# Gated scan and top-1 mixture of experts on one core: the first two pages get their tokens by products with a matrix of ones and zeros, and run on raw fp32 weights

## The chip, the core and the metric

The kernel runs on 1 core of one Trainium2 chip. A core has engines that each run their own list of instructions in order: TensorE (PE, products; its weight loads are PEld), VectorE (DVE), ScalarE (ACT), GpSimd (POOL) and SyncE (SP), which issues most transfers (DMA). The metric is the device time of one execution in microseconds: before the change 928.75 us, the median of 3 runs (927.93 to 928.82).

## The reference

Two stages. The first is a gated linear scan over time, for 4 sequences of 5056 steps and 256 channels; its output is 20224 tokens of 256 numbers. The second sends each token to one of 8 experts.

```python
log_a = c * sig_r * np.log(np.clip(a_base, 1e-06, 1.0 - 1e-06))[None, None, :]
a_t = np.exp(log_a)
norm = np.sqrt(np.maximum(1.0 - a_t * a_t, 1e-06))
x_gated = norm * sig_i * x
for t in range(S):
    h = a_t[:, t] * h + x_gated[:, t]
    y[:, t] = h
...
logits = x @ w_gate + modality_bias[modality_id]
e_idx = np.argmax(logits, axis=1)
...
for e in range(E):
    mask = e_idx == e
    h = np.maximum(x[mask] @ w1[e], 0.0)
    out[mask] = gate_w[mask, None] * (h @ w2[e])
```

An expert is two products, 256 to 1024 and 1024 to 256, with a ReLU between. The bias of the modality decides the expert of nearly every token, so two of the eight experts (the "hot" ones, found on chip from the bias) hold nearly all tokens.

## The kernel before

**Runs.** Time is cut into 23 runs (`RUNS`, called chunks in the code): four of 128 steps, seventeen of 256, and two short ones. A run of 128 steps has 4 x 128 = 512 tokens. For each run: three loads (`load_chunk`: r gate into `a`, i gate into `g`, x into `x`); tanh, exp, square, square root on ACT and the gating on DVE (`scan_chunk`), then the scan itself on DVE (L580); a scale for the run from a sum of squares (`size_chunk`, a small product on PE, L608); a split of the scanned values into a high and a low fp16 half (`split_chunk`, ACT L711 and DVE L714), and the gate logits as products of these halves (PE, L727); the choice of expert and the token's row number (`route_chunk`, DVE, with three small products on PE, L829 to L832: the row number `di` needs how many tokens went to each expert before).

**Rows.** `rows_part` transposes the halves with DMA into a row tile `rt` (SP, L752), one row of 512 fp16 numbers per token with its index and gate value, and POOL scatters these rows to a table `rows` in HBM (L886), 128 tokens a scatter. The table holds each expert's tokens one after the other. A scatter that is recorded after expert products have begun also waits for the PE product recorded last before it (the dependency at the end of `scatter`).

**Pages.** Expert work goes by pages: 256 consecutive rows of one hot expert (later 512, at the end 128). `choose_two` picks one page for each hot expert; `load_rows` reads a page by a transposing DMA (L1206) into `X`, four blocks of 128 x 256 in fp16 (two channel halves, high and low), and the index and gate column into `mt` (L1207). Layer 1 (`first_layer`, L1298) takes, for each block of hidden units, six products of halves (high x high, high x low, low x high, for two channel halves): 48 products of 256 columns a page of 256. ACT and DVE apply the ReLU and split again into `H`; layer 2 (`second_layer`, L1463) is 24 products for each 128 tokens; the result is scaled by the gate and scattered to the output (L1249).

**Weights.** A hot expert's two matrices are loaded in fp32 (`wr`), their scale is worked out (`scale_of`: 16 small products on PE, L339, and one more, L346), and ACT and DVE convert them to a high and a low fp16 half (`convert`, L369 and L375). Pages 0 and 1 (`WHOLE = 2`) are "whole": they keep `H` in fp32 and use the raw fp32 second matrix in layer 2; their first layer uses the fp16 halves.

**What sets the order.** The engines' lists are written by a planner in the program: each piece of work is a generator that asks for an engine for an estimated time, under conditions (`seen`: a mark was reached; `room`: a buffer is free). `run` repeatedly takes the request that can start first, or among near ones that with the best priority (`PRIO`, per run). `PLAN` holds the estimates. `BACKLOG` limits how many tokens the loads run ahead of the pages, `LOOK` and `LOOK_END` how far ahead pages are chosen, `WAIT` when a page is taken up on PE before its data are there, `ROW_STEP` what a later scatter is taken to cost. The planner only sets the order on each engine; on the chip, semaphores set the times.

## Time and profile before

| what | value |
|---|---|
| time, median of 3 runs | 928.75 us |
| the profiled execution's own time | 934.45 us |
| its span | 931.9 us |
| PE busy | 873.1 us, 94% |
| DVE, ACT busy | 662.5 and 662.3 us, 71% each |
| POOL busy | 518.3 us, 56% |
| mean granted clock of PE | 0.991 |

The span is that of the recorded instructions; the execution's time is 2.55 us longer. Busy time says only that an instruction of the engine is under way. The answers of the trace used later are: busy time by stretches, groups of instructions by line (busy us, mean ns of one), the timeline of one engine (start, duration, what), the waits of an engine with what ended them, and the chain of waits that ended last. Where PE's records overlap, the start of one group to the start of the next gives its pace.

### The profile page before, as it was taken

What the parts mean: (1) busy time and instruction counts of PE and PEld (TensorE: products, weight loads), DVE (VectorE), ACT (ScalarE), POOL (GpSimd) and SP (SyncE); (2) the same over time, 40 slices, a digit from 0 to 9 for tenths busy, and PEclk for the clock granted to TensorE, in tenths of its full rate; (3) what the DMA queues carried; (4) which work ended last, traced back from release to release, by engine and by line L of the source; (5) the groups of instructions that cost most, each with busy time, mean ns of one, the idle gap of its engine ahead of it and who ended that gap; (6) DMA issues with size and microseconds to landing.
All of it is one profiled execution on the core that took longest, in us unless ns stands there. A gap on an engine that the chain in (4) does not pass through costs nothing.

```text
span 931.9 us, 22225 instructions
## 1 busy us (share of the span) xinstructions
PE 873.1 (94%) x8453; PEld 775.1 (83%) x8453; DVE 662.5 (71%) x1478; ACT 662.3 (71%) x940; POOL 518.3 (56%) x576
## 2 busy tenths in 40 slices
PE   2399999899799999999999999999999999999996
PEld 2288888798688888888888898888888888888996
DVE  6888687588488778677877887678478667655334
ACT  8977987698688697877888978665376555555343
POOL 5357476578568786776667747755456212221212
PEclk9999999899899999999999999999999999999999
DMA  9999969887776979997798893895473223211230
GB/s 320 235 244 227 234 199 247 216 204 212 212 152 167 284 171 212 219 282 214 199 243 257 193 237 82 182 227 108 104 188 98 63 53 75 52 47 47 58 117 28
DMA packets 223335, 160.96 MB, mean 173 GB/s; under 512 B 197359, under 2 KB 202097, under 8 KB 216690
## 3 DMA queue, kind: packets, MB, share of 16 engines
q1 hardware_dynamic: 206850, 115.20, 53.8%
q0 software_dynamic: 16224, 44.25, 14.6%
q8 instruction: 68, 1.11, 0.5%
q14 instruction: 49, 0.40, 0.1%
q10 hardware_dynamic: 144, 0.00, 0.0%
HBM read 72.96 MB, written 45.01 MB: 127 GB/s over the span
## 4 chain that ended last, share of the span: by engine, by line
PE 84%; issue 5%; DVE 3%; DMA 3%; POOL 2%; ACT 2%; SPq 0%; POOLq 0%; DVEq 0%; ACTq 0%
PE po L1463 42%; PE ph L1298 31%; PE pb L1388 4%; PE pa L1388 3%; PE pc L1388 3%; PE psl L727 2%; DMA wr<-in_moe_w_dram 1%; POOL out_dram L1249 1%; DMA rows<-rt,di 1%; POOL rows L886 0%; DVE x L580 0%; DVE g L554 0%; DMA X<-rows 0%; DVE H L1221 0%; DVE hw L375 0%
## 5 line engine op out<-in xcount | busy, mean ns | idle before, releaser
L1298 PE MATMUL ph<-X,hw 128*128 128x256 f16 (+1 forms) x2880 | 352.4, 273 | 6.2 <-issue 3.8
L1463 PE MATMUL po<-hw,H 128*128 128x256 f16 x2736 | 341.6, 274 | 6.6 <-issue 5.3
L1298 PEld LDWEIGHTS <-hw 128*128 128x128 f16 x2880 | 276.3, 98 | 41.2 <-issue 8.1
L1463 PEld LDWEIGHTS <-H 128*128 128x128 f16 x2784 | 268.7, 98 | 41.1 <-issue 8.2
L886 POOL DMA_INDIRECT rows<-rt,di x158 | 217.2, 1375 | 103.1 <-issue 28.5
L1249 POOL DMA_INDIRECT out_dram<-ot,mt x120 | 146.0, 1217 | 203.2 <-ACT ot L1243 169.9
L1221 DVE SCALAR_TENSOR_TENSOR H<-ph,H 128x512 f16<-128x512 f32 (+1 forms) x240 | 156.4, 667 | 108.0 <-ACT H L1219 82.6
L1219 ACT ACTIVATE H<-ph 128x512 f16<-128x512 f32 (+1 forms) x240 | 137.9, 579 | 117.2 <-PE ph L1298 83.3
L1243 ACT ACTIVATE ot<-po,gt 128x256 f32<-128x256 f32 x160 | 75.1, 472 | 50.8 <-PE po L1463 36.5
L580 DVE TENSOR_TENSOR_SCAN x<-a,x 128x2048 f32<-128x2048 f32 (+2 forms) x23 | 88.1, 3833 | 0.8
L1249 POOL DMA_INDIRECT out_dram<-ot,ids x40 | 49.9, 1248 | 38.3 <-ACT ot L1243 24.6
L1463 PE MATMUL po<-hw,Hx 128*128 128x256 f16 x480 | 68.4, 273 | 0.5 <-ACT Hg L1219 0.5
L566 DVE SCALAR_TENSOR_TENSOR x<-x,g 128x2048 f32<-128x2048 f32 (+2 forms) x23 | 45.9, 1997 | 30.4 <-ACT x L564 22.5
L1463 PE MATMUL po<-hw,Hg 128*128 128x256 f16 x480 | 67.0, 273 | 0.0
L714 DVE SCALAR_TENSOR_TENSOR a<-x,scy,a 128x1024 f16<-128x1024 f32 (+2 forms) x46 | 51.3, 1138 | 2.1 <-ACT a L711 2.1
L1463 PEld LDWEIGHTS <-Hx 128*128 128x128 f16 x480 | 46.8, 98 | 5.9 <-issue 0.6
L1463 PEld LDWEIGHTS <-Hg 128*128 128x128 f16 x480 | 47.0, 98 | 5.4
L1388 PEld LDWEIGHTS <-sw 128*128 128x128 f16 x480 | 47.0, 98 | 5.4
L559 ACT ACTIVATE a<-a,ch 128x1024 f32<-128x1024 f32 (+2 forms) x46 | 50.6, 1119 | 0.1
L711 ACT ACTIVATE a<-x,scy 128x1024 f16<-128x1024 f32 (+2 forms) x46 | 46.1, 1022 | 3.2 <-DVE scy L311 2.0
L554 DVE SCALAR_TENSOR_TENSOR g<-g,x 128x2048 f32<-128x2048 f32 (+2 forms) x23 | 45.8, 1991 | 0.0
L594 ACT ACTIVATE g<-g 128x2048 f32<-128x2048 f32 (+2 forms) x23 | 38.3, 1663 | 4.7 <-DVE x L566 3.4
(226 smaller groups left out, 1110.0 us busy)
## 6 DMA issues: line engine op xcount, KB each, us to landing
a<-in_r_gate_dram SPq DMA_DIRECT2D x17, 1024.0 KB
g<-in_i_gate_dram SPq DMA_DIRECT2D x17, 1024.0 KB
x<-in_x_dram SPq DMA_DIRECT2D x17, 1024.0 KB
wr<-in_moe_w_dram SPq DMA_DIRECT2D x4, 1024.0 KB
cr<-in_moe_w_dram SPq DMA_DIRECT2D x4, 1024.0 KB
a<-in_r_gate_dram SPq DMA_DIRECT2D x5, 512.0 KB
g<-in_i_gate_dram SPq DMA_DIRECT2D x5, 512.0 KB
x<-in_x_dram SPq DMA_DIRECT2D x5, 512.0 KB
```

Of the source, the lines that this page charges most:

```text
L559: nc.scalar.activation(sl, sl, AF.Exp, scale=ch[:, h : h + 1], bias=ch[:, h : h + 1])
L580: nc.vector.tensor_tensor_scan(out=y, data0=a, data1=y, initial=0.0, op0=ALU.mult, op1=ALU.add)
L711: nc.scalar.activation(ys[:, 0, :, u, :], yg[:, :, u, :], AF.Copy, scale=sc)
L714: nc.vector.scalar_tensor_tensor(out=ys[:, 1, :, u, :], in0=yg[:, :, u, :], scalar=sc, in1=ys[:, 0, :, u, :], op0=ALU.mult, op1=ALU.subtract,)
L886: ins = nc.gpsimd.indirect_dma_start(out=rows[:, :], out_offset=bass.IndirectOffsetOnAxis(ap=idx, axis=0), in_=src, in_offset=None, bounds ...
L1219: nc.scalar.activation(hi, src, AF.Relu)
L1221: nc.vector.scalar_tensor_tensor(out=lo, in0=src, scalar=0.0, in1=hi, op0=ALU.max, op1=ALU.subtract)
L1243: nc.scalar.activation(ot, po, AF.Copy, scale=t.gt[:, a : a + 1])
L1249: ins = nc.gpsimd.indirect_dma_start(out=out[:, :], out_offset=bass.IndirectOffsetOnAxis(ap=t.mt[:, a, 0:1] if t.ids is None else t.ids[:, ...
L1298: ins = nc.tensor.matmul(ph[:, v, 0:st], lhsT, rhs, start=(m == 0 and v == 0), stop=(m == len(mm) - 1), skip_group_check=True,)
L1388: ins = nc.tensor.matmul(to[:, v, :], lhsT[s], rhs[x], start=(i in (1, 7) and v == 0 and m == 0), stop=(m == 2), skip_group_check=True,)
L1463: ins = nc.tensor.matmul(prev.po, prev.h(hx, f, rs_), wv[:, wx, f], start=(prev.count == 1), stop=(prev.count == products))
```

## The change

The first run's tokens reach pages 0 and 1 without the table in HBM.

- `choose_pages` now begins with a `choose_two` for run 0 alone, as soon as its tokens have row numbers; before, the first pages were chosen once the scatter of run 0's rows was planned to be done.
- `gather` builds `X` of these pages on chip. For each of the run's 4 columns of 128 tokens, DVE compares the token's place in the page with the numbers 0 to 255 (`place`, a new constant), which gives a 128 x 256 fp16 matrix `to` of ones and zeros. PE multiplies the row tile `rt` with it: 4 products a column (two halves, two channel blocks), 16 a page, summed in one bank, so that high and low are added up. ACT copies the bank to `X`, now 2 blocks in fp32.
- `load_places` still reads index and gate (`mt`) from the table, once run 0's rows are there. The transposing loads `X0` and `X1` fall away.
- Layer 1 of pages 0 and 1 uses the raw fp32 matrix `wr0` or `wr2`: 16 fp32 products a page for 48 fp16 ones. The raw matrix is kept until then, and the gate column is only copied, not scaled.
- `convert` of the four hot matrices stays, for the later pages. The row tile of run 0 is kept until the gathers are done.
- The planner's numbers are others: those below, most of `PRIO` and of `PLAN`. A temporary tile `tie` moves to another pool.

All other pages do the same work; the number of pages and their sizes are as before. Two plain products of 512 columns come in where a bank is first written near the end (`pb`, L1388 before).

The order moves as follows. On DVE, behind the routing of run 0 (`dt0`, `di0`: its row numbers; `x1`: run 1's gating and scan; `hw0_1`: conversion of a second matrix). Before:

```order
L840 TENSOR_TENSOR dt0_479<-psl0_343,be_186 128x32
L845 TENSOR_TENSOR dt0_479<-dt0_479,oh0_457 128x32
L849 TENSOR_REDUCE di0_482<-dt0_479 128x4
L853 TENSOR_TENSOR be_186<-be_186,psl0_343 128x8
L566 SCALAR_TENSOR_TENSOR x1_306<-x1_306,g1_298 128x1024
L375 SCALAR_TENSOR_TENSOR hw0_1_218<-wr1_308,sc1_381,hw0_1_218 128x1024
L574 TENSOR_TENSOR fed1_508<-a1_287,last0_357 128x8
L428 TENSOR_TENSOR hiv0_221<-iv0_320,iv1_382 128x1
L576 TENSOR_TENSOR x1_306<-x1_306,fed1_508 128x8
L578 MEMSET a1_287 128x8
L580 SCALAR_TENSOR_TENSOR x1_306<-a1_287,x1_306 128x1024
```

In the change:

```order
L586 SCALAR_TENSOR_TENSOR x1_310<-a1_291,x1_310 128x1024
L380 SCALAR_TENSOR_TENSOR hw0_1_223<-wr1_337,sc1_403,hw0_1_223 128x1024
L589 COPY last1_518<-x1_310 128x8
L434 TENSOR_TENSOR hiv0_226<-iv0_314,iv1_404 128x1
L312 TENSOR_SCALAR scy1_516<-psl1_513 128x1
L316 TENSOR_SCALAR scy1_516<-scy1_516 128x1
L318 TENSOR_SCALAR ivy1_517<-scy1_516 128x1
L621 TENSOR_TENSOR ivl1_524<-ivy1_517,ivg_233 128x1
L849 TENSOR_TENSOR dt0_527<-psl0_348,be_186 128x32
L854 TENSOR_TENSOR dt0_527<-dt0_527,oh0_442 128x32
L858 TENSOR_REDUCE di0_530<-dt0_527 128x4
L862 TENSOR_TENSOR be_186<-be_186,psl0_348 128x8
```

The row numbers of run 0 stood ahead of run 1's gating and scan; they now stand behind the scan and behind the second half of a conversion. The selection and the eight compares `to` follow them.

On PE, at the first page (`pt3`: scale of the fourth matrix; `psl1`: routing of run 1; `ph0_*`: page 0's layer 1). Before:

```order
L829 MATMUL psl1_525<-oh1_651,um1_163 128x32
L830 LDWEIGHTS ones_161
L830 MATMUL psl1_525<-cu1_653,ones_161 128x32
L832 LDWEIGHTS ones_161
L832 MATMUL psl1_525<-cu1_653,ones_161 128x8
L346 MATMUL pt3_629<-ss3_628,onesf_153 128x1
L608 LDWEIGHTS onesb_157
L608 MATMUL psl2_712<-ssy2_662,onesb_157 128x1
L608 LDWEIGHTS onesb_157
L608 MATMUL psl2_712<-ssy2_662,onesb_157 128x1
L1298 LDWEIGHTS hw0_0_217
L1298 MATMUL ph0_0_747<-X0_0_682,hw0_0_217 128x256
```

In the change:

```order
L838 LDWEIGHTS um1_163
L838 MATMUL psl1_513<-oh1_722,um1_163 128x32
L839 LDWEIGHTS ones_161
L839 MATMUL psl1_513<-cu1_724,ones_161 128x32
L841 LDWEIGHTS ones_161
L841 MATMUL psl1_513<-cu1_724,ones_161 128x8
L1370 MATMUL ph0_1_759<-X0_0_563,wr0_269 128x256 x4
L351 MATMUL pt3_729<-ss3_707,onesf_153 128x1
L1370 MATMUL ph0_2_783<-X0_0_563,wr0_269 128x256 x4
L1370 MATMUL ph0_3_796<-X0_0_563,wr0_269 128x256 x4
L1370 MATMUL ph1_0_814<-X1_0_579,wr2_473 128x256 x4
L1542 MATMUL po0_0_835<-wr1_337,H0_677 128x256 x4
```

Page 0's first layer began behind the routing of run 1; it now begins ahead of it (`ph0_0` stands 20 products ahead of `ph0_1`, of which 17 are for the scales), and the rest of it comes behind the three routing products. Layer 2 of page 0 (`po0_0`) begins, as before, after the first group of page 1.

On SP, before, the part with page 0's load (`rt1`: transposes of run 1; `X0`, `mt0`: page 0's tokens and places):

```order
L752 DMA_TRANSPOSE rt1_0_599<-a1_287 128x4x128 x4
L1201 TENSOR_LOAD sel1_579
L1201 ISA x2
L1206 ISA
L1206 DMA_TRANSPOSE X0_0_682<-rows_78 128x4x256
L1207 ISA
L1207 DMA mt0_681<-rows_78 128x2x2
L522 DMA x3_708<-in_x_dram 128x1024
```

In the change, the part with page 2's load:

```order
L1240 DMA mt1_720<-rows_78 128x2x2
L758 DMA_TRANSPOSE rt1_0_616<-a1_291 128x4x128
L528 DMA g3_747<-in_i_gate_dram 128x1024
L528 DMA x3_774<-in_x_dram 128x1024
L528 DMA a4_830<-in_r_gate_dram 128x2048
L1265 TENSOR_LOAD sel2_841
L1265 ISA x2
L1270 ISA
L1270 DMA_TRANSPOSE X2_0_866<-rows_78 128x4x256
L1271 ISA
L1271 DMA mt2_865<-rows_78 128x2x2
L528 DMA g4_878<-in_i_gate_dram 128x2048
```

Ahead of the last transpose of run 1 there are now the two reads of places, `mt0` and `mt1`, which need run 0's rows in the table; behind it stand three loads and then page 2's tokens, `X2`.

```diff
-WAIT = 2.0
+WAIT = 6.0
...
-BACKLOG = 9000
-LOOK = 256
-LOOK_END = 2944
+BACKLOG = 10500
+LOOK = 384
+LOOK_END = 2432
...
-W_AT = [5, 2, 4, 2]
+W_AT = [10, 3, 6, 2]
...
-ROW_STEP = 2.4
+ROW_STEP = 1.6
...
@@ -209,6 +209,11 @@
     islot = const.tile([P, 2], I32, name="islot")
     nc.gpsimd.iota(islot, pattern=[[P, 2]], base=0, channel_multiplier=1)
     nc.gpsimd.tensor_copy(slot, islot)
+    iplace = sm.tile([P, P], I32, name="iplace", tag="jk", bufs=1)
+    nc.gpsimd.iota(iplace, pattern=[[1, P]], base=0, channel_multiplier=0)
+    place = const.tile([P, 256], F16, name="place")
+    nc.gpsimd.tensor_copy(place[:, 0:P], iplace)
+    nc.gpsimd.tensor_scalar(out=place[:, P:256], in0=place[:, 0:P], scalar1=float(P), scalar2=None, op0=ALU.add)
     pidx = const.tile([P, 1], I32, name="pidx")
     nc.gpsimd.iota(pidx, pattern=[[0, 1]], base=0, channel_multiplier=1)
     quarter = const.tile([P, 1], F32, name="quarter")
...
+            yield "SP", 0.0, seen(("raw1", e)), 0.0
...
-                    rh = rt.bitcast(F16)
+                    rh = tiles["rh", c] = rt.bitcast(F16)
...
             scatter(f"rows{c}", rt[:, u, 0:ROW], di[:, PART * j + u : PART * j + u + 1])
+        end = plan["end"]
+        mark["put", c, j] = end + (PLAN["put"] if c < PLAN["exact"] else 3.0)
+        if c == 0:
+            yield "SP", 0.0, seen(*[("placed", e) for e in range(HOT)]), 0.0
         give("rt", tr)
...
-    def choose_two(size, full, last=False):
+    def choose_two(size, full, last=False, c=None):
 
 
         sel, ticket = new_sel()
-        b2 = tiles["b2", routed(plan["end"]) - 1]
+        b2 = tiles["b2", routed(plan["end"]) - 1 if c is None else c]
...
     def choose_pages():
         other, at = None, FAR
         summed = lambda: max(mark.get(("sw", e), FAR) for e in range(HOT))
+        yield "DVE", 0.16, allof(seen(("route", 0)), room("sel")), 0.0
+        yield from choose_two(256, True, True, 0)
         look = lambda: drained(count["chosen"] - (LOOK if summed() >= FAR else LOOK_END))()
         while True:
...
@@ -1182,6 +1195,51 @@
         yield "POOL", 0.2, None, 0.0
         nc.gpsimd.tensor_tensor(out=t.ids, in0=m, in1=t.mt[:, :, 0], op=ALU.add)
 
+    def gather(t):
+
+        C, r = columns(0), t.pg.e
+        yield "DVE", 0.16, room("X"), 0.0
+        at = sm.tile([P, C], F32, name=f"at{t.n}", tag="at")
+        nc.vector.scalar_tensor_tensor(
+            out=at, in0=t.pg.d[:, r : r + 1].broadcast_to([P, C]), scalar=-256.0, in1=tiles["di", 0], op0=ALU.mult, op1=ALU.add
+        )
+        t.tx.append(take("X"))
+        t.X.append(pm.tile([P, 2, 256], F32, name=f"X{t.n}_0", tag="X", bufs=BUFS["X"]))
+        oh = []
+        for c in range(C):
+            yield "DVE", 0.17, None, 0.0
+            oh.append(sm.tile([P, 256], F16, name=f"to{t.n}_{c}", tag="to", bufs=4))
+            nc.vector.tensor_scalar(out=oh[-1], in0=place, scalar1=at[:, c : c + 1], scalar2=None, op0=ALU.is_equal)
+        for c in range(C):
+            yield "PE", 0.45, allof(room("ph"), seen(("tr", 0, 0))) if c == 0 else None, 0.2 if c == C - 1 else 0.0
+            if c == 0:
+                tp, bank = take_bank(f"pg{t.n}", True)
+            for x in range(2):
+                for k in range(2):
+                    nc.tensor.matmul(
+                        bank[:, k, :], tiles["rh", 0][:, c, x * D + k * P : x * D + (k + 1) * P], oh[c],
+                        start=(c == 0 and x == 0 and k == 0), stop=(c == C - 1 and x == 1), skip_group_check=True,
+                    )
+        mark["placed", r] = plan["end"]
+        if free["ACT"] <= free["DVE"]:
+            yield "ACT", 0.59, None
+            nc.scalar.activation(t.X[0], bank, AF.Copy)
+        else:
+            yield "DVE", 0.68, None
+            nc.vector.tensor_copy(t.X[0], bank)
+        give("ph", tp)
+        t.ready = plan["end"]
+
+    def load_places(t):
+
+        pg, na = t.pg, t.pg.st // P
+        yield "DMA", 0.3, seen(*[("put", 0, j) for j in range(parts(0))]), 0.2
+        src = nc.sync.value_load(pg.sel[0:1, pg.col : pg.col + 1], min_val=0, max_val=NULLS + WIDE - pg.size)
+        sel_read(pg)
+        t.mt = pm.tile([P, na, 2], I32, name=f"mt{t.n}", tag="mt", bufs=10)
+        read_rows(pg, nc.sync.dma_start(t.mt, rows[ds(src, pg.st), D:].rearrange("(a p) m -> p a m", p=P)))
+        mark["places", t.n] = plan["end"]
+
     def load_rows(n=0):
         while True:
             while n >= len(pages):
@@ -1189,7 +1247,13 @@
                     return
                 yield "SP", 0.0, lambda: 0.0 if len(pages) > n or count["ended"] else FAR, 0.0
             pg = pages[n]
-            if True:
+            if n < HOT:
+                t = Tile()
+                t.pg, t.n, t.X, t.tx, t.ready, t.ids = pg, f"{pg.n}", [], [], FAR, None
+                queue.append(t)
+                add(gather(t), (0, 3), plan["end"], urgent=True)
+                add(load_places(t), (0, 2), plan["end"])
+            else:
                 st, na = pg.st, pg.st // P
                 t = Tile()
                 t.pg, t.n, t.X, t.tx = pg, f"{pg.n}", [], []
...
         if t.pg.e is None:
             return max(t.ready, mark.get(("cw", t.pg.c), FAR))
+        if t.pg.n < HOT:
+            return max(t.ready, mark.get(("got", 2 * t.pg.e), FAR))
...
             tp, ph = take_bank(f"ph{cur.n}_{g}", st == 256)
-            w1v = (pg.w if pg.e is None else hw[pg.e])[0].rearrange("p (s k f) -> p s k f", s=2, k=2)
+            if pg.n < HOT:
+                wf = raw2[pg.e, 0][0].rearrange("p (k f) -> p k f", k=2)
+            else:
+                w1v = (pg.w if pg.e is None else hw[pg.e])[0].rearrange("p (s k f) -> p s k f", s=2, k=2)
             for v in range(2):
                 f = 2 * g + v
                 fs = slice(f * P, (f + 1) * P)
-                mm = [
-                    (w1v[:, s, k, fs], cur.X[0][:, 2 * x + k, :])
-                    for k in range(2) for s, x in ((0, 0), (0, 1), (1, 0))
-                ]
+                if pg.n < HOT:
+                    mm = [(wf[:, k, fs], cur.X[0][:, k, :]) for k in range(2)]
+                else:
+                    mm = [
+                        (w1v[:, s, k, fs], cur.X[0][:, 2 * x + k, :])
+                        for k in range(2) for s, x in ((0, 0), (0, 1), (1, 0))
+                    ]
                 for m, (lhsT, rhs) in enumerate(mm):
...
             for g in range(4):
-                yield 1.312 * st / 256, [room("ph")] + ([ready, room("H")] if g == 0 else []), lambda g=g: plain(g), 0.25
+                yield 1.75 if pg.n < HOT else 1.312 * st / 256, [room("ph")] + ([ready, room("H")] if g == 0 else []), lambda g=g: plain(g), 0.25
...
             if begins:
                 conds.append(room("po"))
+                if prev.pg.n < HOT:
+                    conds.append(seen(("places", prev.n)))
                 if a // 2 not in prev.to:
                     conds.append(room("ot"))
                 if pg.e is not None and not prev.to:
-                    conds.append(seen(("got", 2 * pg.e + 1), ("w", 2 * pg.e)) if prev.whole else seen(("hot", pg.e)))
+                    conds.append(seen(("got", 2 * pg.e + 1), *([] if pg.n < HOT else [("w", 2 * pg.e)])) if prev.whole else seen(("hot", pg.e)))
             yield "PE", (0.45 if prev.whole else 0.328) * len(run_), allof(*conds), 0.0
             if not prev.to:
                 gates = prev.mt[:, :, 1].bitcast(F32)
                 prev.gt = sm.tile([P, st // P], F32, name=f"gt{prev.n}", tag="gt", bufs=3)
-                nc.vector.tensor_scalar(out=prev.gt, in0=gates, scalar1=pg.inv if pg.e is None else tiles["wiv", 2 * pg.e] if prev.whole else hiv[pg.e], scalar2=None, op0=ALU.mult)
+                if pg.n < HOT:
+                    nc.vector.tensor_copy(prev.gt, gates)
+                else:
+                    nc.vector.tensor_scalar(out=prev.gt, in0=gates, scalar1=pg.inv if pg.e is None else tiles["wiv", 2 * pg.e] if prev.whole else hiv[pg.e], scalar2=None, op0=ALU.mult)
             if begins:
                 if a // 2 not in prev.to:
                     prev.to[a // 2] = take("ot")
```

More of the change, by code (lines that the diff above doesn't have):

```diff
@@ L54 @@
 EARLY = 7
-ROW_STEP = 2.4
+ROW_STEP = 1.6
 LAG = 2.5
-PLAN = dict(dma=3.6, b0=0, b1=16, b2=0, b3=24, put=1.5, hold=1, cold=20, ls=4.4, lr=0.14, ll=0.16, lc=0.36, dma0=0.5, l1=12, l4=24, exact=9, w0=6, w1=4, w2=4, w3=6, land=2, xland=3, row=1.55, beside=9, op=0.13, gprio=0, oh=0.1, lag=1.5, latefrom=8, h=(0, 0), o=(0, 4))
+PLAN = dict(dma=3.6, b0=5.6, b1=20, b2=8.4, b3=20, put=1.5, hold=1, cold=5, ls=4.4, lr=0.09, ll=0.16, lc=0.42, dma0=1.0, l1=12, l2=20, l3=34, l4=28, exact=5, w0=6, w1=3, w2=6, w3=6, land=2, xland=3, row=1.3, beside=9, op=0.13, gprio=0, oh=0.1, lag=2, latefrom=8, h=(0, 0), o=(0, 4), convkey='route', convhold=(1, 0, -1, -1), sumhold=(0, 1, -1, 1))
 def lag_of(c):
@@ L147 @@
     cmp = const.tile([1, E, E], F32, name="cmp")
-    tie = const.tile([1, E, E], F32, name="tie")
+    tie = sm.tile([1, E, E], F32, name="tie", tag="ex")
     nc.vector.tensor_tensor(out=tie, in0=keyt.broadcast_to(one8), in1=key.broadcast_to(one8), op=ALU.is_equal)
@@ L774, in rows_part @@
             scatter(f"rows{c}", rt[:, u, 0:ROW], di[:, PART * j + u : PART * j + u + 1])
+        end = plan["end"]
+        mark["put", c, j] = end + (PLAN["put"] if c < PLAN["exact"] else 3.0)
+        if c == 0:
+            yield "SP", 0.0, seen(*[("placed", e) for e in range(HOT)]), 0.0
         give("rt", tr)
-        mark["put", c, j] = plan["end"] + (PLAN["put"] if c < PLAN["exact"] else 3.0)
     def route_chunk(c):
@@ L1031, in choose_two @@
             pg = new_page(size, e, sel, e, not full)
+            if c is not None:
+                pg.routed, pg.d = c + 1, d
             pg.ticket = ticket, left
@@ L1304, in plain @@
             if g == 3:
+                if pg.n < HOT:
+                    mark["raw1", pg.e] = plan["end"]
                 for tx in cur.tx:
@@ L1444, in second_layer @@
                 prev.gt = sm.tile([P, st // P], F32, name=f"gt{prev.n}", tag="gt", bufs=3)
-                nc.vector.tensor_scalar(out=prev.gt, in0=gates, scalar1=pg.inv if pg.e is None else tiles["wiv", 2 * pg.e] if prev.whole else hiv[pg.e], scalar2=None, op0=ALU.mult)
+                if pg.n < HOT:
+                    nc.vector.tensor_copy(prev.gt, gates)
+                else:
+                    nc.vector.tensor_scalar(out=prev.gt, in0=gates, scalar1=pg.inv if pg.e is None else tiles["wiv", 2 * pg.e] if prev.whole else hiv[pg.e], scalar2=None, op0=ALU.mult)
             if begins:
```

2 lines of the change are left out of this document (1 added, 1 removed).

## The prediction

> **What bounds the kernel now.** I read the busy times first, then the same by stretches, then TensorE's waits, then the chain of waits.
>
> ```profile
> PE 873.1 (94%) x8453; PEld 775.1 (83%) x8453; DVE 662.5 (71%) x1478; ACT 662.3 (71%) x940; POOL 518.3 (56%) x576
> ```
>
> TensorE (PE) is busy for 94% of the span. By stretches (us; busy time of PE, PEld, DVE, ACT, POOL; then granted clock, DMA share, GB/s):
>
> ```profile
> 0.00:48.00 48.00, 13.09 (x119) 10.92 (x120) 35.85 (x123) 42.86 (x53) 23.27 (x100) 1.00 0.94 273
> 48.00:81.00 33.00, 33.00 (x255) 28.17 (x255) 27.88 (x72) 27.14 (x36) 19.57 (x25) 1.00 0.93 239
> 162.00:176.00 14.00, 10.71 (x94) 8.02 (x93) 6.49 (x17) 6.90 (x9) 7.75 (x13) 0.76 0.90 227
> 249.00:924.00 675.00, 667.95 (x6559) 597.79 (x6558) 478.43 (x1036) 460.70 (x690) 362.51 (x329) 1.00 0.62 154
> 924.00:932.00 8.00, 0.33 (x4) 0.05 (x1) 0.00 (x0) 0.47 (x1) 0.98 (x1) 0.79 0.06 17
> ```
>
> PE idles for 35 us before 48, then hardly at all until 924. Its waits say the same (line, what ended the wait: us, times, longest):
>
> ```profile
> PE psl L727 <- issue: 5.2, 9, 1.2
> PE ph L1298 <- DMA X<-rows: 2.2, 1, 2.2
> PE po L1463 <- DVE H L1221: 1.1, 2, 0.6
> ```
>
> Once, at page 0, it waits for tokens. So a change of the start is worth what it moves PE's unbroken stretch, less the PE work it puts into that stretch. The chain of waits into page 0 (start, us, what):
>
> ```profile
> 35.85 1.97 POOL rows L886
> 38.13 6.39 DMA rows<-rt,di
> 44.53 3.40 DMA X<-rows
> 47.97 8.36 PE ph L1298 x60
> ```
>
> The last scatter of run 0, its 6.39 us to land and the 3.40 us load are what the change takes out.
>
> **The change, part by part.** *PE's prices.* PE's timeline:
>
> ```profile
> 39.26 1.87 PE L339 MATMUL pt<-wr 128*128 128x128 bf16 x16
> 56.16 1.89 PE L1463 MATMUL po<-wr,H 128*128 128x256 f32 x8
> 57.89 1.47 PE L1298 MATMUL ph<-X,hw 128*128 128x256 f16 x12
> 59.20 1.89 PE L1463 MATMUL po<-wr,H 128*128 128x256 f32 x8
> 75.01 0.55 PE L727 MATMUL psl<-wg,a 128*128 128x16 f16 x16
> 80.34 1.47 PE L1298 MATMUL ph<-X,hw 128*128 128x256 f16 x12
> ```
>
> Start to start, four fp32 products (eight records) take 57.89 - 56.16 = 1.73 us, 0.433 each; twelve fp16 ones 59.20 - 57.89 = 1.31, 0.109 each. Layer 1 of the two pages: 96 x 0.109 = 10.5 us go, 32 x 0.433 = 13.9 come. The gathers add 32 x 0.109 = 3.5, the two plain products of 512 columns near the end 4 x 0.109 = 0.4.
>
> *A cold PE.* Groups of page 0's products in 49 to 50 and in 52.6 to 53.4 us (busy, mean ns):
>
> ```profile
> L1298 PE MATMUL ph<-X,hw 128*128 128x256 f16 x6 | 1.5, 421 | 0.0
> L1298 PE MATMUL ph<-X,hw 128*128 128x256 f16 x10 | 1.3, 272 | 0.0
> ```
>
> The first products go at half pace: 60 took 8.36 us instead of 6.5. I take the same 1.8 us for the gathers, which come first in the change; the 32 column-sum products behind them then cost half of row 39.26's pace, 1.75 us together. The Trainium skill (TensorE: Matmul & The Clock Gate, section "What's actually happening") says that the array's clock is halved after an idle window and released after about 3.4 us of sustained work, a time and not a number of products. That speaks against the change, which puts more products into the cold time; by it the gathers lose about 1.7 us, and without it the start would come out that much better. The trace agrees: half pace from 47.97 to about 51.4.
>
> *When the gathers begin.* The DVE's and ACT's rows:
>
> ```profile
> 25.99 1.13 ACT L369 ACTIVATE hw<-wr,sc 128x1024 f16<-128x1024 f32 x1
> 28.44 1.15 ACT L564 ACTIVATE x<-x,quarter 128x1024 f32<-128x1024 f32 x1
> 29.14 0.21 DVE L849 TENSOR_REDUCE di<-dt 128x4 int32<-128x32 f32 x1
> 29.62 1.23 DVE L566 SCALAR_TENSOR_TENSOR x<-x,g 128x1024 f32<-128x1024 f32 x1 [0.20 <-ACT x L564]
> 30.76 1.28 DVE L375 SCALAR_TENSOR_TENSOR hw<-wr,sc,hw 128x1024 f16<-128x1024 f32 x1
> 32.38 2.44 DVE L580 TENSOR_TENSOR_SCAN x<-a,x 128x1024 f32<-128x1024 f32 x1
> ```
>
> Run 0's row numbers are ready at 29.4 before; the change puts them behind run 1's scan and a conversion. On ACT the root of run 1 now stands ahead of the conversion of row 25.99, so the gating of row 29.62 comes about 1.5 us earlier, at 28.1. From there: gating 1.15, conversion 1.2, small steps 0.4, scan 2.3, conversion 1.2, six scale steps 0.7, row numbers and totals 1.0, selection 0.6, place 0.15: 36.8. A compare of 128 x 256 is not in the trace; below it lies a compare-sized step of 128 x 16 elements, above it half of one of 128 x 512:
>
> ```profile
> 10.29 0.23 DVE L661 TENSOR_SCALAR wg<-wg,scg 128x16 f16<-128x16 f32 x1
> 59.40 0.69 DVE L1232 TENSOR_SCALAR H<-ph 128x512 f32<-128x512 f32 x1 [1.52 <-PE ph L1298]
> ```
>
> So 0.1 (a small step's start-to-start share) to 0.35 us each; I take 0.2, nearer the small one, since the operands are fp16 in SBUF. The first gather begins at **37.0**; with no gain on ACT and slow compares at 39, with quick small steps at 36. The eight compares (1.6 us) hide behind the gathers (5.3 us), or at 0.35 nearly so.
>
> *From there to the end of page 2's layer 1* PE has: gathers 3.5 + 1.8; column sums 1.75 and two closing products 0.4; logits of runs 1 and 2 0.8; small products 0.2; fp32 layers 1 and 2 of both pages 13.9 + 13.9; page 2's layer 1 48 x 0.109 = 5.2. Sum 41.4, so 78.4. The routing of run 1 that now stands inside page 0 needs DVE until about 45.5, and PE reaches it at 46.4, so it costs only its products. ACT's copy of a bank (0.6) hides behind the column sums. Before, that point is 80.34, less 0.45 for run 3's logits and routing, which the change has later: 79.9. **The start gains 1.5 us; less 0.4 for the two products, 1.1.** With the bounds of the gathers' begin: -0.9 to +2.1. Dropping two of 82 page loads and the two adds on POOL frees nothing that PE waited for; the longer lives of `wr0`, `wr2` and `rt0` delay no load that is not already issued.
>
> *What is late next.* Page 2's tokens. Their scatters each wait for the product recorded before them, the last one for the end of page 1's first group, in the list above four fp32 groups after the routing; POOL's and SP's rows of run 1 before:
>
> ```profile
> POOL rows L886 <- PE ph L1298: 25.5, 26, 2.1
> 52.49 1.84 POOL L886 DMA_INDIRECT rows<-rt,di  x1 [0.30 <-issue]
> 59.57 1.25 SPq L1206 DMA_TRANSPOSE X<-rows  x1
> ```
>
> Last scatter to page load 7.1 us, plus 3.4 to land: 10.5. PE has seven fp32 groups, 12.1 us, between the same two points, a margin of 1.6. But SP's list also holds the last transpose of run 1 behind `mt0`, which needs run 0's rows: scatters from 36.3 to about 41.8, landing 6.4, two reads 0.9, the transpose about 3.4 give 52.5 for run 1's first scatter, against 48.1 by the products; then page 2 is 1.8 late. I take the middle, 0, as both orders of events are possible.
>
> The planner's other numbers move runs and loads by a few groups in the middle, where PE waits for no run; I take 0. The profiled execution (934.45) lies 5.7 above the median, so its stalls are not all in the timed runs: I set the sum on the median, 928.75 - 1.1 = **927.6**.
>
> **The rivals.**
>
> *A. A stall of the middle goes.* SP's list before run 6:
>
> ```profile
> 151.74 0.35 SPq L522 DMA_DIRECT2D a<-in_r_gate_dram  x1
> 152.19 0.38 SPq L522 DMA_DIRECT2D g<-in_i_gate_dram  x1
> 158.87 7.95 SPq L752 DMA_TRANSPOSE rt<-a  x4
> ```
>
> In 162 to 176 (row above) PE did about 6.1 us of work in 13.1: waits that nothing in the profile ends, then half clock; DVE and ACT stand at half too. SP had just issued two loads of 1024 KB ahead of run 6's transposes; the change moves one behind them. For it: the place; against: other such stretches lie where nothing moves. If the half clock alone goes (24 products at twice 0.109: 2.6), 925.0; if all 6.9 goes, 920.7. I say 923.5.
>
> *B. The row numbers come sooner.* If DVE reaches them at 34 instead of 36 (each of some fifteen small steps 0.1 us quicker than I count) and PE's routing of run 1 is no later, another 1.5 us: 926.1.
>
> *C. Page 2's or page 4's tokens are late.* Page 4 before:
>
> ```profile
> 85.44 1.25 SPq L1206 DMA_TRANSPOSE X<-rows  x1
> 96.26 4.09 PE L1298 MATMUL ph<-X,hw 128*128 128x256 f16 x36
> ```
>
> Run 2's last scatter now stands behind page 2's second layer; by the same count page 4 is left with 10.6 us of PE work for 10.5 of transfers. With 2 us more for a landing at both places PE waits 1.8 + 2 at the first and 2 at the second: 5.8 - 1.1, **933.4**. It decides from 3 us of waits on. Against it: before, page 4's load was issued 10.8 us ahead of its use, so it was ready some 7 us early. That the early pages bring nothing at all, as `X` is early but page 2 takes all of it back, is the forecast's upper end, 928.8.
>
> **How the numbers follow.** Forecast 0.38, A 0.25, B 0.17, C 0.20. What this kernel's measurement tells from no change is 0.2%, 1.9 us. Forecast (its own range 926.6 to 929.6) is "same" up to its ends; A and B are faster, C slower. So faster 0.42, same 0.37, slower 0.21. The predicted time is the forecast's, 927.6. The range takes in B, A's middle and its far end nearly, and C's first place alone (928.75 - 1.1 + 3.8 = 931.5): 921.0 to 931.5.
>
> **What would show it.** First gather at 36 to 39 and the end of page 2's layer 1 near 78.4; gathers at 421 ns, then 272; no PE wait on `X<-rows` over 1 us. For A, no clock below 0.9 near 162 to 176. For B, the first gather before 36. For C, PE waiting for `X<-rows` at pages 2 or 4. The forecast is wrong if PE is not unbroken from the gathers on, or if the time moves while the end of page 2's layer 1 does not.

## The result, and the profile after

The changed kernel takes **940.77 us** (median of 4 runs, 938.09 to 942.59) against 928.79 for the kernel before (4 runs, 927.93 to 929.92): ratio 1.0139, 95% interval 1.0095 to 1.0183. It is 12 us slower. The forecast was 927.6, and its range ended at 931.5. Below, an execution that lay far above the others of its kernel is left out of median and ratio.

TensorE's busy time and records in the page after:

```profile
PE 880.9 (94%) x8455; PEld 779.1 (83%) x8455; DVE 664.4 (71%) x1488; ACT 662.8 (71%) x942; POOL 519.5 (55%) x575
```

TensorE by three stretches that are the same in both (us; busy time and records, granted clock, DMA share, GB/s), first before, then after:

```profile
48.00:81.00 33.00, 33.00 (x255) 1.00 0.93 239
81.00:120.00 39.00, 38.03 (x373) 1.00 1.02 252
120.00:705.00 585.00, 569.79 (x5613) 0.99 0.81 198
```

```profile
48.00:81.00 33.00, 33.00 (x210) 1.00 0.86 226
81.00:120.00 39.00, 34.78 (x342) 0.96 0.87 209
120.00:705.00 585.00, 567.35 (x5576) 0.99 0.81 203
```

Up to 81 us TensorE is unbroken, as forecast. Then come two places that the forecast left at nothing: 4.2 us of idle time between 81 and 120 (before: 1.0), and 17.7 between 120 and 705 (before: 15.2, in an execution that lay 5.7 us above the median). TensorE's waits after the start (what ended them; us, times, longest) say what kind they are:

```profile
PE po L1542 <- issue: 7.0, 16, 1.0
PE ph L1370 <- issue: 4.5, 8, 1.3
PE po L1542 <- DVE H L1285: 3.4, 2, 2.0
PE psl L838 <- DVE oh L827: 1.0, 1, 1.0
```

The `issue` rows are stalls that no wait explains. The other two are true waits; but for 1.3 us behind 400 us they lie in the first stretch. The timeline of TensorE, ACT and DVE there (start, duration, what; in brackets the idle time ahead of it and what ended it):

```profile
36.71 5.38 PE L1219 MATMUL pg<-to,rt 128*128 128x256 f16 x32 [5.64 <-DVE to L1212]
78.48 1.47 PE L1370 MATMUL ph<-X,hw 128*128 128x256 f16 x12
92.49 0.39 PE L1542 MATMUL po<-hw,H 128*128 128x256 f16 x2 [0.93 <-ACT x L570]
94.94 4.86 PE L1542 MATMUL po<-hw,H 128*128 128x256 f16 x28 [2.05 <-DVE H L1285]
```

```profile
89.95 2.00 ACT L570 ACTIVATE x<-x,quarter 128x2048 f32<-128x2048 f32 x1
91.86 0.58 ACT L1283 ACTIVATE H<-ph 128x512 f16<-128x512 f32 x1
```

```profile
91.99 2.29 DVE L572 SCALAR_TENSOR_TENSOR x<-x,g 128x2048 f32<-128x2048 f32 x1 [1.33 <-ACT x L570]
94.19 0.68 DVE L1285 SCALAR_TENSOR_TENSOR H<-ph,H 128x512 f16<-128x512 f32 x1
```

The start went as worked out: the first gather at 36.71, and the last group that the sum counts ends where the next begins, at 78.48 (forecast 78.4). At 92 us TensorE wants the last quarter of page 3's hidden layer. Its rectifier stands behind run 4's square root in ACT's list and its second half behind run 4's gating in DVE's, so TensorE gets it at 94.9. Behind the two waits the 28 products take 4.7 us, start to start, in place of 3.1. The Trainium skill (TensorE: Matmul & The Clock Gate, section "What's actually happening") says that an idle window halves the array's clock until it has been busy again for about 3.4 us; the granted clock of 0.96 over this stretch agrees.

### The profile page after: what moved, and what is told of

Same layout as the page of the kernel before. It is cut to its first block, busy times and chain, and to the rows that moved or that the text cites. A ratio compares the mean times of both kernels' runs of the same rounds, so it can differ in the third digit from the quotient of the medians.

```text
span 940.0 us, 22221 instructions
## 1 busy us (share of the span) xinstructions
PE 880.9 (94%) x8455; PEld 779.1 (83%) x8455; DVE 664.4 (71%) x1488; ACT 662.8 (71%) x942; POOL 519.5 (55%) x575
## 5 line engine op out<-in xcount | busy, mean ns | idle before, releaser
L1542 PE MATMUL po<-hw,H 128*128 128x256 f16 x2736 | 345.3, 275 | 11.9 <-issue 7.0
L1370 PE MATMUL ph<-X,hw 128*128 128x256 f16 (+1 forms) x2784 | 339.4, 272 | 4.8 <-issue 4.5
L1370 PEld LDWEIGHTS <-hw 128*128 128x128 f16 x2784 | 265.8, 98 | 38.7 <-issue 7.8
L895 POOL DMA_INDIRECT rows<-rt,di x158 | 220.2, 1394 | 104.7 <-issue 36.2
```

The source lines that it names most:

```text
L895: ins = nc.gpsimd.indirect_dma_start(out=rows[:, :], out_offset=bass.IndirectOffsetOnAxis(ap=idx, axis=0), in_=src, in_offset=None, bounds ...
L1370: ins = nc.tensor.matmul(ph[:, v, 0:st], lhsT, rhs, start=(m == 0 and v == 0), stop=(m == len(mm) - 1), skip_group_check=True,)
L1542: ins = nc.tensor.matmul(prev.po, prev.h(hx, f, rs_), wv[:, wx, f], start=(prev.count == 1), stop=(prev.count == products))
```

## The experiments

Up to four kernels at a time ran on one chip, with the kernel before on the same chip. A single edit is shown against the changed kernel unless it says otherwise.

**The same two kernels on other chips.** e5 is the kernel before, e6 and e12 are the changed kernel, none of them edited.

> The kernel before once more, unchanged, for a trace from the chip on which these runs are made: the comparison of traces so far is between two profiled executions of another chip, and there the one of before lay 5.7 us over its own median, with two stalls of 7 and 8.5 us at 162 and 232 us that no wait explains. If those stalls belong to that chip or that execution, this trace has none and PE's waits add to less than 5 us after the start; if they belong to the kernel, they stand at the same places.

> The changed kernel once more, unchanged, beside the kernel before on this chip. Ratio 1.010 to 1.018 if the loss is the kernel's own. If the loss of the first comparison came from stalls without a wait (13.6 us of PE's idle time in its trace), which the other chip hardly shows, the ratio is 1.000 to 1.008.

> The changed kernel once more beside the kernel before, for the chip on which the next two are made. If the loss of the first comparison (12 us) belongs to that chip, the ratio is 1.002 to 1.004 again; if it depends on the hour or on chance, it can be anywhere from 1.002 to 1.018, and then this trace has stalls of TensorE that no wait explains.

| chip | kernel before, us | changed kernel, us | ratio, 95% interval |
|---|---|---|---|
| of the first comparison | 928.79 | 940.77 | 1.0139 (1.0095 to 1.0183) |
| of e5 to e7 (e15, e16 later: 909.32 before) | 909.25 | 911.45 | 1.0028 (1.0018 to 1.0037) |
| of e12 to e14 | 925.98 | 937.39 | 1.0132 (1.0109 to 1.0155) |
| of e1 to e4 / e8 to e11 / e17, e18 | 909.01 / 909.57 / 909.46 | not run | |

Chips differ: on a quicker one (909 us) the loss is 2.2 us, on a slower one (926 to 929) 11 to 12. The first comparison does not name its chip, so it may be that of e12 to e14. The trace on the quicker chip separates the two causes, since it has no stall without a wait. TensorE by stretches, e5 and then e6:

```profile
81.00:120.00 39.00, 39.00 (x387) 1.00 0.99 264
120.00:705.00 585.00, 584.53 (x5836) 1.00 0.84 201
```

```profile
81.00:120.00 39.00, 35.55 (x364) 1.00 0.83 205
120.00:705.00 585.00, 584.56 (x5836) 1.00 0.83 206
```

Nothing is lost behind 120 us, in either kernel. The 3.45 us between 81 and 120 are the changed kernel's own. Of these the start gives back about 1. The waits of e6 that make them up:

```profile
93.30 3.23 PE L1542 MATMUL po<-hw,H 128*128 128x256 f16 x28 [1.29 <-DVE H L1285]
104.74 0.51 PE L733 MATMUL psl<-wg,a 128*128 128x16 f16 x14 [1.01 <-DVE a L720]
111.52 0.19 PE L838 MATMUL psl<-oh,um 128*128 128x64 f16 x1 [1.01 <-DVE oh L827]
```

All three wait on run 4: for the group held up behind its gating, for its scaled values (its logits), for its choice of expert. In the trace after, the first of them is 2.98 us in two parts, with half clock behind it: there ACT stands 1.50 us for a product of TensorE ahead of run 4's root, which e6 does not show.

**Numbers or structure.** e1 is the changed code with all of the planner's numbers as before, e2 the code before with all of the new numbers, e3 and e4 take back one table each.

```diff
e1  WAIT, BACKLOG, LOOK, LOOK_END, W_AT, PRIO, ROW_STEP, PLAN: as before
e2  (kernel before) the same eight: as in the change
e3  PRIO: as before
e4  PLAN: as before
```

> The changed kernel with all of the planner's numbers (WAIT, BACKLOG, LOOK, LOOK_END, W_AT, PRIO, ROW_STEP, PLAN) as they were before; the gathers, the raw fp32 layers and the early routing of run 0 stay. Theory N (the numbers cost the time: the order that they give ACT, DVE and SP after the start makes PE wait, first for the last group of page 3's first layer): the loss is gone, 926 to 930. Theory S (the new work itself costs it: gathers, fp32 layers, the rows of run 0 held on chip): still 938 to 942. Under a mixture, where the numbers fit the new start and the old ones do not, it is slower than 930 for a reason of its own, and PE's waits show at another place.

> The kernel before with all of the changed planner's numbers and nothing else of the change. Theory N: most of the 12 us comes with the numbers, 937 to 943. Theory S: 927 to 931, as the kernel before.

> The changed kernel with the table PRIO alone as before. Theory N, with the table as the main number, since it sets which run's steps stand ahead of a page's first layer on DVE and ACT: 927 to 933. If the numbers of PLAN carry it, or theory S: 937 to 943. The static order still has run 4's gating ahead of the last group of page 3 on DVE, so a wait of PE for H of about 5 us near 90 us can stay.

> The changed kernel with the dictionary PLAN alone as before (the planner's costs and due times of loads). Theory N with PLAN as the main number: 927 to 933. If PRIO carries it, or theory S: 937 to 943. Here DVE has run 4's gating ahead of the last but one group of page 3.

| kernel | time, us | ratio, 95% interval |
|---|---|---|
| e1, new code, old numbers | 943.55 | 1.0375 (1.0361 to 1.0389) |
| e2, old code, new numbers | 931.26 | 1.0249 (1.0235 to 1.0263) |
| e3, old PRIO | 924.00 | 1.0170 (1.0151 to 1.0189) |
| e4, old PLAN | 918.35 | 1.0096 (1.0081 to 1.0112) |

Neither theory N nor S, but the third case of e1's expectation: every mixture is slower than the changed kernel's 1.0028 on such a chip. The numbers and the code fit each other, and a misfit costs more than the change does. In e1 the next page's tokens are late, by rival C's mechanism: TensorE stands for them for 15 us.

```profile
125.51 4.85 PE L1370 MATMUL ph<-X,hw 128*128 128x256 f16 x22 [15.34 <-DMA X<-rows]
```

The mixtures also show what each part does to run 4. Its gating on DVE, in e5 (old code, old numbers), e1 (code alone), e2 (numbers alone) and e6 (both):

```profile
83.83 2.29 DVE L566 SCALAR_TENSOR_TENSOR x<-x,g 128x2048 f32<-128x2048 f32 x1 [0.97 <-ACT x L564]
```

```profile
86.55 2.29 DVE L572 SCALAR_TENSOR_TENSOR x<-x,g 128x2048 f32<-128x2048 f32 x1 [2.62 <-ACT x L570]
```

```profile
92.26 2.29 DVE L566 SCALAR_TENSOR_TENSOR x<-x,g 128x2048 f32<-128x2048 f32 x1 [2.99 <-ACT x L564]
```

```profile
90.35 2.29 DVE L572 SCALAR_TENSOR_TENSOR x<-x,g 128x2048 f32<-128x2048 f32 x1 [1.82 <-ACT x L570]
```

The code alone makes it 2.7 us later, the numbers alone 8.4, both 6.5. So each part makes it later, but they do not add up, and the share of each in the change stays open. What the code adds can be read from e6 at the start. ACT's and DVE's rows:

```profile
40.31 0.60 ACT L1226 ACTIVATE X<-pg 128x512 f32<-128x512 f32 x1 [4.91 <-PE pg L1219]
40.81 0.81 ACT L565 ACTIVATE a<-a,ch 128x512 f32<-128x512 f32 x1
46.33 1.15 ACT L570 ACTIVATE x<-x,quarter 128x1024 f32<-128x1024 f32 x1
```

```profile
37.75 0.29 DVE L1212 TENSOR_SCALAR to<-place,at 128x256 f16<-128x256 f16 x1 [0.58 <-PE pg L1219]
40.52 1.41 DVE L720 SCALAR_TENSOR_TENSOR a<-x,scy,a 128x512 f16<-128x512 f32 x2
```

ACT stands 4.9 us for the first page's bank, with run 2's exponentials queued behind it; run 2's root comes at 46.3, where e5 has it at 40.4:

```profile
40.42 1.15 ACT L564 ACTIVATE x<-x,quarter 128x1024 f32<-128x1024 f32 x1
```

DVE stands four times for 0.53 to 0.58 us, because the second page's compares wait for the four buffers of the first, with run 1's scaling behind them. No run takes away ACT's wait, so that it is what makes run 4 later is argued and not shown.

**Run 4.** e7 and e8 exchange two pairs of neighbours, so that page 3's group goes ahead of run 4; all other rows stay. In e7 run 4's squares of g also overtook the gating, which then worked on squared values; e8 keeps the computation.

```diff
 ACT
+H3<-ph3_3
 x4<-x4,quarter      (root)
-H3<-ph3_3
 DVE
+H3<-ph3_3,H3
 x4<-x4,g4           (gating)
-H3<-ph3_3,H3
```

> The changed kernel with two pairs of neighbours exchanged and every other row of every engine's list as it was: on ACT the rectifier of page 3's last group goes ahead of run 4's square root, on DVE the same group's rest goes ahead of run 4's gating. Theory Q (PE stands at 92 us because this group waits in ACT's and DVE's lists behind run 4): the waits of 0.9 and 2.05 us and the half clock behind them go, 3 to 5 us less than the changed kernel beside it, and PE's progress at 100 us is as at 80 us. Theory R (the time comes back at the next late step, since run 4's scan is no earlier): 0 to 2 us less, and the wait for the routing of run 4 near 113 us grows from 1.0 us to 3 to 5 us.

> The exchange of the run before this one with the computation kept: on ACT the rectifier of page 3's last group goes ahead of run 4's root, on DVE the same group's rest ahead of run 4's gating, and run 4's squares stay behind the gating, which they had lost; all other rows of all lists stand as in the changed kernel. On a chip like the last the changed kernel lies 2.2 us over the one before (0.28%). Theory Q (page 3's group is held up by its place in the lists): PE's wait of 1.3 us at 93 us goes and with it 1.3 to 2 us of the time. Theory R (run 4 itself is late: its root, gating, scan and scaling end when they end, and PE stands for its logits and its routing next): the wait at 93 goes, those at 104 and 111 us (1.0 each) grow by as much, and the time is the changed kernel's within 0.5 us.

e7: 916.01 us, ratio 1.0076 (1.0063 to 1.0089), not a clean measure. e8: 913.81 us, 1.0048 (1.0035 to 1.0061). Theory Q falls: the wait for the group went, and others came, for run 4 again:

```profile
97.62 0.16 PE L619 MATMUL psl<-ssy,onesb 128*128 128x1 bf16 x1 [1.22 <-ACT g L605]
107.12 0.51 PE L738 MATMUL psl<-wg,a 128*128 128x16 f16 x14 [1.18 <-DVE a L725]
```

In e8 ACT stands 1.59 us for page 3's products ahead of run 4's root, and run 4's gating begins at 93.24 where e6 has it at 90.35; 0.7 us of this stands ahead of it already. So this exchange only hands the delay on to run 4. It is even 0.2% slower than the changed kernel, where theory R expected the same time.

e9 shortens run 4's chain, e10 lengthens it, e14 lengthens it in the kernel before.

```diff
e9, run 4 only
-sqrt(x4); x4 = max(x4, ..) * g4
+sqrt(x4[first half]); sqrt(x4[second half])
+x4[first half] = max(..) * g4; x4[second half] = max(..) * g4
e10, e14, run 4 only
+nc.scalar.activation(y, a, AF.Square)
 nc.scalar.activation(y, a, AF.Square)
```

> The changed kernel with run 4's root and gating each issued as two halves, so that DVE gates the first half while ACT takes the root of the second: run 4's scan starts about 1.0 us sooner at 0.1 to 0.2 us more work on each engine; nothing else moves. Theory R (run 4's chain sets PE between 88 and 112 us): 0.7 to 1.0 us less than the changed kernel. If another chain sets it: no change.

> The changed kernel with run 4's square before the root taken twice (the same values, 1.9 us more on ACT at about 86 us). Theory R: PE's waits at 93, 104 and 111 us grow by 1.5 to 1.9 us together and the time by as much. If run 4 has slack: less than 0.5 us.

> The kernel before with run 4's square taken twice, as was done to the changed kernel (there 1.9 us more on ACT cost about 3 us). If run 4 has slack before and none after, which is the step that the prediction left at nothing: within 0.5 us of the kernel before, ratio 0.9995 to 1.0005 or so. If run 4's chain sets PE in both, 1.5 to 3 us more.

e9: 910.83 us, 1.0018 (1.0009 to 1.0027). e10: 914.61 us, 1.0057 (1.0045 to 1.0069). e14, on a slower chip: 928.87 us, 1.0035 (1.0014 to 1.0055). TensorE's first wait for run 4 in e9, e10 and e14:

```profile
93.13 3.23 PE L1544 MATMUL po<-hw,H 128*128 128x256 f16 x28 [0.47 <-DVE H L1287]
```

```profile
95.69 4.90 PE L1543 MATMUL po<-hw,H 128*128 128x256 f16 x28 [2.10 <-DVE H L1286]
```

```profile
95.75 3.88 PE L1464 MATMUL po<-hw,H 128*128 128x256 f16 x34 [1.91 <-DVE H L1222]
```

Half the root's time sooner, and the wait falls from 1.29 to 0.47 us (ahead of it TensorE and ACT both stand 0.65 us later than in e6, so the two waits can be compared). 1.9 us more on ACT, and it grows to 2.10 beside a wait of 0.96 ahead of it, with half clock behind both; the time grows by some 2.6 us (0.29% between its ratio and that of e6). That agrees with theory R: run 4's chain, and what stands behind it in ACT's and DVE's lists, sets TensorE here. But e14 did not come out as its first case expected: the kernel before pays for the same 1.9 us too, with 0.35%. The group that TensorE waits for in e14 stands right behind run 4's scan in DVE's list:

```profile
90.56 4.42 DVE L581 TENSOR_TENSOR_SCAN x<-a,x 128x2048 f32<-128x2048 f32 x1
95.01 1.28 DVE L1222 SCALAR_TENSOR_TENSOR H<-ph,H 128x512 f16<-128x512 f32 x2
```

So run 4, with what is queued behind it, has hardly any slack before either; it is only just in time.

e11 gives the compares eight buffers, e13 and e17 both helpful edits.

```diff
e11
-to: four buffers of 128 x 256 for both pages
+to: four for page 0, and for page 1 one output buffer that holds four
e13, e17 = e11 + e9
```

> The changed kernel with eight buffers for the matrices of ones and zeros instead of four (the second page's four lie in a buffer of the output rows, not yet in use). In the changed kernel DVE stands 0.57 us four times at 37 to 40 us, because the second page's compares wait for the first page's products, and run 1's scaling and run 2's first gating stand behind them. These waits (2.25 us) go. Theory S (the start's waits in DVE's list are what makes runs 2 to 4 late): run 4's gating comes 1 us or more sooner and the time is 1 to 2 us less. Theory T (ACT's list, which stands 4.9 us for the first page's bank ahead of run 2's exponentials, and PE's pace after that set the runs): run 4's gating moves by less than 0.5 us, and so does the time.

> The changed kernel with both helpful edits: eight buffers for the matrices of ones and zeros, and run 4's root and gating in halves. The two act at different places (36 to 45 us, 88 to 95 us), so their gains should add: 0.7 and 0.8 us less than the changed kernel, about 0.7 us over the one before, ratio 1.000 to 1.002. If the start's gain is taken back where PE stands for run 4, as the time of the first edit alone hints, only 0.8 us less.

> The changed kernel with eight buffers for the matrices of ones and zeros and with run 4's root and gating in halves, once more, hoped for on a quicker chip: there the changed kernel lies 0.28% over the one before and each of the two edits took 0.7 to 0.8 us of TensorE's progress. If they add: ratio 1.000 to 1.002, and progress at 120 us 1.3 to 1.5 us better than the changed kernel's. If it is a slower chip, the ratio is 1.009 to 1.014 as before and says nothing.

e11: 912.04 us, 1.0027 (1.0018 to 1.0037), no change in the time, as theory T has it. Run 4's gating comes 0.66 us sooner in its trace (89.69), which lies between the bounds of T and S; unedited executions of the changed kernel differ by 0.2 to 0.5 us there. e13, on a slower chip: 938.28, 1.0129 (1.0083 to 1.0175), which says nothing. e17: 911.31, 1.0025 (1.0013 to 1.0036). The gains do not add up in the time, and no version came out below the kernel before. e9's 0.1% is itself not clear of the changed kernel's interval; for run 4 the waits carry the argument, not that time.

**Stalls without a wait, on the slower chips.** In the trace after, TensorE at 195 us, and POOL at the same time:

```profile
195.31 0.27 PE L1370 MATMUL ph<-X,hw 128*128 128x256 f16 x1 [0.21 <-issue]
196.04 0.27 PE L1542 MATMUL po<-hw,H 128*128 128x256 f16 x1 [0.45 <-issue]
196.75 0.27 PE L1542 MATMUL po<-hw,H 128*128 128x256 f16 x1 [0.44 <-issue]
```

```profile
194.30 0.98 POOL L895 DMA_INDIRECT rows<-rt,di  x1 [0.30 <-issue]
195.58 0.97 POOL L1313 DMA_INDIRECT out_dram<-ot,ids  x1 [0.30 <-issue]
196.86 0.97 POOL L895 DMA_INDIRECT rows<-rt,di  x1 [0.31 <-issue]
```

One to four products every 0.71 us, for six microseconds, and then half clock. On the quicker chip the same place of the program (e6) has the same spacing of scatters, and TensorE goes on unbroken:

```profile
190.63 0.97 POOL L1313 DMA_INDIRECT out_dram<-ot,ids  x1 [0.30 <-DMA rows<-rt,di]
191.91 0.97 POOL L895 DMA_INDIRECT rows<-rt,di  x1 [0.30 <-issue]
```

```profile
192.42 1.47 PE L1542 MATMUL po<-hw,H 128*128 128x256 f16 x12
193.73 1.47 PE L1370 MATMUL ph<-X,hw 128*128 128x256 f16 x12
```

Two executions of one kernel have the same rows in every list, so the delay of one behind the other can be read row by row. The trace before lies 1.1 us behind e5 at 120 us and 25.4 at 700; the trace after lies 2.2 us behind e6 at 120 and 30.6 at 700 (ACT's row `sv<-pb`, L1405, starts at 753.10 in the one and at 722.46 in the other). Six stalls of over 0.5 us of idle time, with the half clock behind them, make up 21.9 of the 24.3 us that the trace before loses between; in the trace after, eight of them make up 25.7 of 28.5 (e12: six, 14.1 of 18.6). Most of their places recur: in the times of e6's rows, the traces after, e12 and e13 all stall at 192 to 195, 305, 330 and 627 us; in those of e5's rows, the traces before and e14 both stall at 162 to 163, 295 and 567. The chip decides whether they come at all. The load of the transfers does not tell these places apart: over 11 us around each stall in the trace after the DMA share lies between 0.31 and 1.06, and its mean from 120 to 705 us is 0.81.

In the five traces from slower chips (before, after, e12, e13, e14) there are 30 such stalls behind 120 us. Each begins with 3 or 4 scatters issued in the 5 us ahead; of the time between 120 and 700 us that holds for 37 to 45%. And the change has longer rows of scatters: in e5 and e6, counting a row as scatters less than 1.65 us apart behind 120 us, 10 and 17 rows of five or more, and 43 and 64 scatters beyond the third of their row. The two counts have ratios of 1.7 and 1.5. What the slower chips add to the time has about the same ratio: 19.5 us before and 29.3 after on the first (928.79 - 909.25 and 940.77 - 911.45), 16.7 and 25.9 with e12. The rows alone are not enough, since on the quicker chips they pass without a stall. e15 and e16 space the scatters by a small step on POOL, in the changed kernel and in the kernel before; e18 takes back the planner's cost of a scatter.

```diff
e15, e16, behind every scatter from the thirteenth on
+nc.gpsimd.tensor_scalar(out=t, in0=t, scalar1=1.0, scalar2=None, op0=ALU.mult)
e18
-ROW_STEP = 1.6, PLAN row=1.3
+ROW_STEP = 2.4, PLAN row=1.55
```

> The changed kernel with a small step on POOL (128 x 128, fp16, about 0.55 us) behind every scatter from the thirteenth on; all other rows of all lists stand as they were. The traces of two chips on which the kernel before takes 926 to 929 us show stalls of TensorE without a wait, and each of them begins some 5 us into a row of scatters that POOL issues back to back, 1.3 us apart, with 3 to 4 in the 5 us ahead of it where the mean is 2.1; on the three chips where it takes 909 us there is none. Theory B (on the slower chips such rows of scatters hold TensorE up, and the change has more of them): on a slower chip the step spaces them to 1.9 us, the stalls fall by half or more, and the ratio to the kernel before falls from 1.013 to 1.008 or less; on a quicker chip it stays at 1.002 to 1.006, as later scatters bring only small waits. Theory C (the stalls have nothing to do with the scatters): on a slower chip 1.013 or more.

> The kernel before with the same step behind every scatter from the thirteenth on. Theory B: on a slower chip it is quicker than the kernel before, by 3 to 10 us, on a quicker chip 0 to 3 us slower. Theory C: 0 to 3 us slower on either.

> The changed kernel with the planner's costs of a scatter as they were (ROW_STEP 2.4 instead of 1.6, and 1.55 instead of 1.3 for the early runs). The planner then spaces the scatters wider, but every list moves with it, as with each number so far. Theory B (rows of back-to-back scatters): fewer rows of five and more than the changed kernel's 17, and on a slower chip a ratio of 1.010 or less if the new order has no waits of its own. Theory N (numbers and structure fit one another, and one old number among the new ones is a misfit): slower than the changed kernel by 3 to 12 us on a quicker chip, as with the old PRIO and the old PLAN.

All three fell on quicker chips. e15: 1003.0 us, 1.1031 (1.1009 to 1.1053); e16: 987.71 us, 1.0859 (1.0841 to 1.0877). e15 is 92 us slower than the changed kernel on that chip, e16 78 us slower than the kernel before, where small waits were expected. So they say nothing of the stalls, but much of POOL. The step and TensorE's waits in e16:

```profile
L889 POOL TENSOR_SCALAR junk<-junk 128x128 f16<-128x128 f16 x326 | 249.3, 765 | 11.0
```

```profile
PE ph L1306 <- DMA X<-rows: 26.9, 6, 8.9
PE po L1471 <- DVE H L1228: 18.2, 8, 7.2
```

Scatters that come 0.8 us later each make tokens late. e18: 923.37 us, 1.0147 (1.0131 to 1.0162), with 9 rows of five or more in place of 17, and waits of its own (6.2 us for `H`): again one old number among the new ones is a misfit. Whether fewer rows help on a slower chip was not seen.

## Why the prediction was wrong

**The start was right.** The first gather came at 36.71 (forecast 37.0), half pace in the gathers cost what was set down, the sum ended at 78.48 (78.4), and TensorE did not wait for page 2's or page 4's tokens: the middle value 0 for page 2 held, and rival C did not come. The start gains about 1 us, on the quicker chip too.

**The step that failed** is "The planner's other numbers move runs and loads by a few groups in the middle, where PE waits for no run; I take 0." It is wrong twice. The row behind it is that PE waited for no run *before*; it does not say that the runs had slack, and e14 shows that run 4 had hardly any. And run 4's gating moves by 6.5 us (e6), five groups of 1.3 us; the numbers alone move it by 8.4 (e2), the code alone by 2.7 (e1). That is the 3.45 us between 81 and 120, and, with the start's gain, the 2.2 us on the quicker chips (e6), where 1.1 us less was forecast; e9 and e10 move these waits both ways by changing run 4's steps alone.

**A smaller miss of the same kind**: "ACT's copy of a bank (0.6) hides behind the column sums", and "the eight compares (1.6 us) hide behind the gathers". TensorE did not wait for either. But the copy waits 4.9 us at the head of ACT's list, with run 2's exponentials behind it, and the compares wait 2.3 us in DVE's. What is queued behind a waiting instruction was asked for page 2's tokens and not for these. By e1 the code makes run 4 2.7 us later; by e11 the compares' share of it costs nothing.

**What no term held**: about 9 of the 12 us appear only on the slower chips. About 1 of them comes between 81 and 120 us, where the delay of the trace after behind e6 grows by 2.4 us and that of the trace before behind e5 by 1.5. The rest lies behind 120 us, where nine tenths of what the slower chip adds to these two traces are stalls without a wait, which the quicker chips' traces have not. How much more of them the change has rests on the medians: one execution of the changed kernel lies 30.6 us behind e6 (after), another 19.6 (e12). The prediction knew such stalls (rival A) and asked which of them would go; it did not ask whether the change would bring more. Rival A's stall did go, as this row of the stretches after shows, and another came at 195:

```profile
162.00:176.00 14.00, 14.00 (x157) 1.00 0.92 222
```

That the longer rows of back-to-back scatters bring such stalls fits in place and in size, but was not shown: no run that spaces the scatters fell on a slower chip. Why TensorE stalls at these places, and on some chips only, stays open.

**The profile of before** was 5.7 us above its median, so it overstated the stalls; the same holds the other way for e12's trace (930.99 against a median of 937.39). So the split into 2.2 and 9 rests on times from several chips, not on one pair of traces.

## What to carry to other kernels

An engine that waits for nothing is no proof that its suppliers have slack: before a reordering is taken at nothing, read how long ahead of its use each supplier ended, and what stands behind every new wait in its own engine's list. In a kernel whose order is written by a planner, the numbers and the code are one thing; undoing either, in whole or in part, gave here a time 1 to 4% over the kernel before, and told more of the fit than of the part. And measure a change of this size on more than one chip.

## What the runs showed of the hardware that was not expected

The chip matters more than the change: the same kernel before takes 909.0 to 909.6 us on four chips and 926.0 to 928.8 on one or two others, and the traces put most of the difference into stalls of TensorE that no wait explains, mostly at the same places of the program. In the one shown its products come every 0.71 us.

POOL has less room than its 55% of busy time suggests: a step of its own behind each scatter, 0.77 us in the mean, cost 78 us in the kernel before and 92 in the changed one. And part of its busy time is standing still. A scatter that takes 0.98 us in the rows above does not end before DVE's scan when one runs (e6):

```profile
121.65 4.33 POOL L895 DMA_INDIRECT rows<-rt,di  x1 [0.30 <-issue]
```

```profile
120.77 4.42 DVE L586 TENSOR_TENSOR_SCAN x<-a,x 128x2048 f32<-128x2048 f32 x1
```

The Trainium skill (SBUF — State Buffer, section "Who interferes with whom") says that a DVE instruction with two inputs in SBUF, as the scan has, keeps out a GpSimd instruction that reads there, as the scatter reads its row numbers. The trace agrees: 4.33 us in place of 0.98. In e6 all 16 scatters of over 2 us beside such a scan end 0.78 to 0.82 us behind its end; the 66 that begin beside `H<-ph,H`, which has one input in SBUF and one in a bank, take 0.98 us in the median.
